# Eleven units' planes added on VectorE, filter weights loaded in two row groups, the last half tile in two parts, a zeroed tile for TensorE, and new order strings

## The chip, the cores and the metric

The kernel runs on one core of one Trainium2 chip. The core has five engines that run their own instruction queues in order and wait for each other through semaphores: TensorE (PE, matrix multiplications and transposes into PSUM), VectorE (DVE), ScalarE (ACT), GpSimd (POOL) and SyncE (SP, here the engine that issues nearly all DMA transfers). The metric is the device time of one execution in microseconds.

## The reference, cut to what matters

One block with two branches, batch 1, 2048 positions (S), 640 features (D), 1728 hidden features (F), all tensors bf16. The first branch is a spectral filter (a two-dimensional real Fourier transform over positions and features, a product with a complex weight, and the inverse), the second a gated feed-forward network. Both are modulated by six vectors that come from a condition `c`.

```python
mod = (silu(c) @ w_mod).reshape(1, 6, 1, 640)
sa, ca, ga, sb, cb, gb = (mod[:, i] for i in range(6))

h = layernorm(x) * (1 + ca) + sa
X = rfft2(h, axes=(1, 2)) * (w_r + 1j * w_i)       # [2048, 321] complex
x = x + ga * irfft2(X, s=(2048, 640), axes=(1, 2))

h = layernorm(x) * (1 + cb) + sb
x = x + gb * ((silu(h @ w_gate) * (h @ w_up)) @ w_down)
return x
```

## The kernel before, in words

The 2048 positions are 16 tiles of 128. The work has four stages, which follow each other on TensorE with some overlap. Inside the first three, the order of the work is written out by hand as a string (`plan`): each word is a step and a number, and the program issues the steps in that order, so that the string fixes the order on every engine's queue and on the DMA queue. PSUM is handed out in slots; the strings `SLOTS1` (three slots in stage 1) and `SLOTS2` (four slots afterwards) say which slot the next tile takes, and a matmul that writes a slot waits until the slot's last reader is done.

**Stage 1, forward transform.** For each tile `t` the steps are: `T` transposes x on TensorE (five 128x128 pieces), `h` copies them out, `G` forms sums of squares on TensorE, `d` (line 313) takes the statistics on VectorE, `p`/`r` root and reciprocal, `s` (line 333) scales a table `Gtab` on GpSimd, `B` multiplies with the table for the feature transform (line 340), `Z` (line 345) takes that out of PSUM on VectorE, `S` (lines 353, 354) does the position transform, `A` (line 367, tile 12 lines 362 to 364) copies the result to `A_sb`. At the end come the steps that prepare the weights and the shift: `ms`, `sacs`, `mh`, `sh` for the vector `sa`; `J`/`Je` (lines 438, 443) which reverse the weights on TensorE and copy them out to `Wq`; `N` (line 278) which negates three blocks on VectorE. The filter weights come in by `lW` (one DMA for each of the two tensors, 128 rows of 16x321), and `lf` (line 210) then overwrites parts of row 0 with eight small DMAs. `J` and `N` read the result.

**Stage 2, filter.** The transformed data are 17 units (0 to 16, the last one small). For a unit: `T`/`t` or a DMA transpose (`B`, `Bl`, line 487 and 492) brings `A_sb` into the order of the columns; `X` (lines 523 to 531) multiplies on TensorE for two units at a time, `Xe` (line 540; unit 16: line 536) copies it out of PSUM; `P` and `R` (both line 562) multiply with the weights on VectorE and leave two planes; `Y` turns the planes back on TensorE, `y` (line 599) copies it out; `E` (lines 611 to 624) multiplies on TensorE and `e` (line 634; half of unit 15 is `g15`) copies to `Ep`; `m` (line 278) writes negated mirror columns of `Ep` on VectorE.

For `Y` there are two ways. Without addition, TensorE multiplies each plane with the identity and sums both in PSUM: ten matmuls of 128 columns (lines 586 and 590), fp32 in PSUM. For the units in `ADDED`, VectorE adds the two planes first (`a`, line 570) and TensorE only transposes the sum: five transposes (lines 580 and 581), bf16 in PSUM.

Which engine copies a tile out of PSUM is decided by its name: names in `ON_DVE` go to VectorE, all others to ScalarE (`evict`).

**Stage 3, inverse transform and start of the network.** `s` (line 720), `V` (line 727), `d` (line 733) and `x` (line 736) undo the transform and form the residual x1; then come the second normalisation, its transposes, and for the first 512 positions the first eight of 13 blocks of the network (`g`, line 812, `z`, line 817, `m`, line 821). `w`, line 848, multiplies a row block of `w_down` with the gate; those blocks that are not in the string come in the loop behind it by `folds`.

**Stage 4, network.** Four groups of 512 positions, 13 blocks and a short 14th each, then the product with `w_down`: `down` (line 934) runs 13 matmuls into one accumulator of 128x320 for each half tile, `down13` (line 921) adds the short block, `x_out` (lines 946, 948) adds the residual and sends the tile out (lines 950, 952). The very last half tile has two accumulators of 160 columns; the residual is put into them by two identity matmuls (line 931), their matmuls alternate, and at the end ScalarE copies one and VectorE the other, and one DMA sends the 320 columns.

At the start TensorE waits for the first transfer (`c`), does five tiny matmuls with it (line 398) and twelve matmuls of the identity whose result is not used (line 400).

Of the kernel before, what the change touches and what calls it, by code (L numbers as in the profile page):

```python
# [30 lines left out]
def _tables():  # L31
# [79 lines left out]
def adaln_block_kernel(  # L111
# [39 lines left out]
    one11 = const.tile([1, 1], BF16, name="one11")  # L151
    identb = const.tile([P, 128], BF16, name="identb")
# [29 lines left out]
    g_row = [dram.tile([1, D], BF16, name=n) for n in ("ga_row", "gb_row")]  # L182
    nc.vector.memset(one11[:], 1.0)
# [34 lines left out]
    def load_g(g):  # L218
# [4 lines left out]
             "lW": lambda a: nc.sync.dma_start(Wb[:, a, :, 0:321], ws[a]), "lK": load(Ktab[:], K_dram), "lKI": load(KIt[:], KI_dram),  # L223
# [3 lines left out]
        "A12 Xe0 Xe9 Xe10 Xe16 e1 e14 e15 f0 f1 f2 f3 f4 f6 f7 f8 f9 g15 h0 t0 t1 y0 y2 y4 y8 y12 y14 y16 "  # L227
# [55 lines left out]
    with tc.tile_pool(name="ph1", bufs=3) as ph1, \  # L283
# [111 lines left out]

        cps = Tt[:, 330:330 + NC5]
        for k in range(NC5):
            nc.tensor.matmul(cps[:, k:k + 1], lhsT=c_row[0:1, k * 128:(k + 1) * 128], rhs=one11[:], start=True, stop=True)
        for _ in range(12):
            nc.tensor.matmul(Gt[:, 0:128], lhsT=identb[:], rhs=identb[:], start=True, stop=True)  # L400
# [44 lines left out]
        def negate(i):  # L445
# [30 lines left out]
    with tc.tile_pool(name="ph2", bufs=2, reuse_waits="tile") as ph2:  # L476
# [186 lines left out]
        def loads(i):  # L663
# [44 lines left out]
    def ring(name):  # L708
        return take2(name)
# [140 lines left out]
    def at_of(sc):  # L850
# [31 lines left out]
    folds = {8: (4, 5, 6), 9: (7,), 10: (8,), 11: (9, 10, 11), 12: (12, 13)}  # L882
    for sc in range(4):
# [3 lines left out]
        for fc in range(0 if sc else done, NFC - 1):  # L887
# [30 lines left out]
        def down13(tl, h):  # L918
            r = slice(64 * h, 64 * h + 64)
# [102 lines left out]
```

## Time and profile before

| | |
|---|---|
| median of 3 runs | 262.87 us (262.04 to 264.65) |
| the profiled execution, its own time | 262.81 us |
| span in the profile | 261.0 us |
| TensorE busy | 252.7 us (97%) |
| VectorE busy | 141.1 us (54%) |
| ScalarE busy | 118.6 us (45%) |
| GpSimd busy | 26.4 us (10%) |
| moved by DMA | 27.88 MB |

The profile is of one execution. Its span reaches from the first to the last recorded event; 1.8 us of the execution's time lie outside of it. The page has the busy time of each engine, the chain of work that ended last, followed back through what released each instruction, and the groups of instructions by line. The trace behind it can be asked for windows, for one engine's instructions in order of time, and for what each waited for. The ends of matmuls are modelled: a matmul's duration includes its way through the array, while the next one starts long before. So the step from one start to the next says what a matmul costs in a row.

### The profile page before, as it was taken

The numbers are of one execution on the slowest core, as the hardware profiler recorded it, in microseconds if no ns is written. First come the engines' busy times: TensorE is split into PE (matmuls) and PEld (weight loads), VectorE is DVE, ScalarE is ACT, GpSimd is POOL, SyncE is SP. The second block draws the span as 40 slices with busy tenths as digits, with TensorE's granted clock in tenths as the row PEclk, the third lists the DMA queues.
The fourth block names the chain that finished last, engine by engine and source line by source line (L and its number), as shares of the span: only waits on it lengthen the run. The fifth ranks groups of instructions, "written<-read, shape, count | busy, mean of one in ns | idle before, by whom it ended". The sixth has DMA issues, their size and how long they took to land.

```text
span 261.0 us, 5283 instructions
## 1 busy us (share of the span) xinstructions
PE 252.7 (97%) x2168; PEld 159.9 (61%) x2172; DVE 141.1 (54%) x353; ACT 118.6 (45%) x212; POOL 26.4 (10%) x57
## 2 busy tenths in 40 slices
PE   6899999999999999999999999999999999999995
PEld 5788666888995444466544456744445664444664
DVE  5799989999887664933243343234344322433122
ACT  5689879996993669420222222032223103222000
POOL 4289700000010001300000000000000000000000
PEclk9999999999999999999999999999999999999999
DMA  7999499999599100141100040210005011000011
GB/s 243 381 356 298 112 175 160 176 330 379 153 370 303 38 14 1 23 77 57 58 10 3 0 92 11 75 35 10 3 0 100 30 48 35 10 3 0 0 53 50
DMA packets 36798, 27.88 MB, mean 107 GB/s; under 512 B 19493, under 2 KB 34214, under 8 KB 36646
## 3 DMA queue, kind: packets, MB, share of 16 engines
q1 hardware_dynamic: 36762, 27.54, 37.1%
q8 instruction: 17, 0.28, 0.5%
q14 instruction: 7, 0.06, 0.1%
q10 hardware_dynamic: 12, 0.00, 0.0%
HBM read 20.13 MB, written 2.62 MB: 87 GB/s over the span
## 4 chain that ended last, share of the span: by engine, by line
PE 79%; DVE 12%; ACT 3%; issue 2%; DMA 2%; SPq 1%; DVEq 0%; ACTq 0%
PE gu L812 37%; PE oa L934 21%; PE va L720 3%; DVE PP L562 3%; DMA x_sb<-in_A_x_dram 2%; PE oab L733 2%; PE gu L799 2%; ACT junk L744 2%; PE aps L353 1%; DVE AT L821 1%; PE aps L354 1%; PE z L340 1%; DVE Z L345 1%; PE gps L308 1%; DVE late L848 1%
## 5 line engine op out<-in xcount | busy, mean ns | idle before, releaser
L821 DVE TENSOR_TENSOR AT<-gu,sg 128x512 bf16<-128x512 f32 x52 | 35.7, 690 | 63.3 <-ACT sg L817 63.3
L812 PE MATMUL gu<-h2T_all,Wg 128*128 128x512 bf16 x260 | 64.6, 379 | 0.1
L812 PE MATMUL gu<-h2T_all,Wu 128*128 128x512 bf16 x256 | 63.7, 379 | 0.1
L817 ACT ACTIVATE sg<-gu 128x512 f32<-128x512 f32 x52 | 30.7, 596 | 67.9 <-PE gu L812 65.1
L934 PE MATMUL oa<-late,AT 128*128 128x320 bf16 x403 | 56.3, 299 | 0.5 <-DVE AT L821 0.5
L934 PEld LDWEIGHTS <-AT 128*128 128x128 bf16 x429 | 40.7, 98 | 17.6 <-issue 1.1
L812 PEld LDWEIGHTS <-Wu 128*128 128x128 bf16 x260 | 25.4, 98 | 30.7
L812 PEld LDWEIGHTS <-Wg 128*128 128x128 bf16 x260 | 25.3, 98 | 29.9
L948 DVE TENSOR_TENSOR xo<-oa,late 128x320 bf16<-128x320 f32 x31 | 13.4, 484 | 34.6 <-PE oa L934 18.2
L801 ACT ACTIVATE sg<-gu 64x512 f32<-64x512 f32 x4 | 2.4, 591 | 36.0 <-PE gu L799 36.0
L736 DVE SCALAR_TENSOR_TENSOR late<-oab,x_sb 128x640 bf16<-128x640 f32 x16 | 12.8, 822 | 6.4 <-PE oab L733 5.0
L333 POOL TENSOR_SCALAR Gs<-Gtab,rstd 128x256 bf16<-128x256 bf16 x15 | 13.9, 928 | 8.1 <-DVE rstd L323 7.1
L345 DVE SCALAR_TENSOR_TENSOR Z<-rtile,vm,z 128x640 bf16<-128x640 f32 x16 | 13.9, 871 | 0.1
L744 ACT ACTIVATE junk<-late,mean 128x640 bf16<-128x640 bf16 x16 | 13.3, 828 | 0.3
L367 ACT CAST A_sb<-aps 128x650 bf16<-128x650 f32 x15 | 10.6, 706 | 2.1 <-PE aps L354 2.0
L727 ACT CAST VT<-va 128x640 bf16<-128x640 f32 x16 | 10.2, 699 | 1.9 <-PE va L720 1.8
L720 PE MATMUL va<-Htab,Ep 128*128 128x128 bf16 x160 | 10.6, 219 | 0.1
L720 PEld LDWEIGHTS <-Ep 128*128 128x128 bf16 x160 | 9.5, 118 | 0.4 <-DVE Ep L278 0.3
L353 PE MATMUL aps<-Z,Gs 128*128 128x325 bf16 x32 | 9.2, 303 | 0.2 <-DVE Z L345 0.2
L354 PE MATMUL aps<-Z,Gs 128*128 128x315 bf16 x32 | 9.2, 298 | 0.0
L540 ACT CAST X<-xps 128x640 bf16<-128x640 f32 x13 | 8.5, 710 | 1.1 <-PE xps L531 0.8
L562 DVE TENSOR_TENSOR PP<-X,Wb 128x768 bf16<-128x768 bf16 x16 | 8.7, 550 | 0.0
(291 smaller groups left out, 307.0 us busy)
## 6 DMA issues: line engine op xcount, KB each, us to landing
x_sb<-in_A_x_dram SPq DMA_DIRECT2D x8, 320.0 KB
out_dram<-xo SPq DMA_DIRECT2D x15, 160.0 KB, 2.2
Wu<-in_B_w_up_dram SPq DMA_DIRECT2D x1, 2080.0 KB
late<-in_B_w_down_dram SPq DMA_DIRECT2D x1, 2080.0 KB
wm_g<-in_w_mod_dram SPq DMA_DIRECT2D x2, 800.0 KB
Wb<-in_A_w_r_dram SPq DMA_DIRECT2D x1, 1284.0 KB
Wb<-in_A_w_i_dram SPq DMA_DIRECT2D x1, 1284.0 KB, 13.0
Wg<-in_B_w_gate_dram SPq DMA_DIRECT2D x1, 1280.0 KB, 8.1
```

Source lines behind the costliest of these rows:

```text
L333: e.tensor_scalar(Gss[t][:, 0:2], Gtab[:, t], rstd1[:, t:t + 1], None, ALU.mult)
L345: nc.vector.scalar_tensor_tensor(Zs[t][:].rearrange("p r q -> p (r q)"), rv, vm[:, t, 1:2], held.pop(("z", t))[:, 0:D], ALU.mult, ALU.add)
L353: nc.tensor.matmul(o, lhsT=Gs[:, a, :], rhs=Z[:, :, 0:NL], start=True, stop=False)
L562: nc.vector.tensor_tensor(bass.AP(o.tensor, o.offset, [o.ap[0], [4 * NI, 2], [2 * NI, 2], [4, n], [1, 4]]), bass.AP(xi.tensor, xi.offset, ...
L720: nc.tensor.matmul(vf[:, 128 * r:128 * r + 128], lhsT=Ep[:, t, 65 - 65 * g:193 - 65 * g, r], rhs=Htab[:, t, g, :], start=(f == 1 and r in ...
L736: nc.vector.scalar_tensor_tensor(x1[:, t, :].rearrange("p (a r) -> p a r", r=NR), VTs.pop(t).rearrange("p (r a) -> p a r", r=NR), 1.0, x_s ...
L744: nc.scalar.activation(junk[:], x1[:, t, :], ACT.Square, scale=-1.0 / D ** 0.5, bias=mean2[:, t, 1:2], accum_out=sq2[:, t:t + 1])
L812: nc.tensor.matmul(o, lhsT=w_[:, c5, fc * 128:(fc + 1) * 128], rhs=h2T(sc, c5), start=(c5 == 0), stop=(c5 == NC5 - 1))
L817: nc.scalar.activation(gus[fc][1][:], gus[fc][0][:, 0, :], ACT.Silu)
L821: nc.vector.tensor_tensor(AT[:, fc, :], gu[:, 1, :], sg[:], ALU.mult)
L934: nc.tensor.matmul(o, lhsT=AT[:, fc, tl * 128:(tl + 1) * 128], rhs=Wd_sb[:, fc, h * 320 + d0:h * 320 + d0 + n], start=(fc == 0 and not ear ...
L948: nc.vector.tensor_tensor(xos[tl][:, h * 320:(h + 1) * 320], ps[0][0], x_half(tl, h), ALU.add)
```

## The change

1. `ADDED` goes from eight units (0, 2, 4, 6, 8, 10, 12, 14) to eleven (1, 2, 4, 5, 6, 8, 9, 10, 12, 13, 14).
2. `ON_DVE` is another set. In stage 1, `A11` and `h3` are copied by VectorE instead of `A12` and `h0`. In stage 2 VectorE gives up `Xe0`, `Xe9`, `Xe10`, `Xe16`, `e1`, `e14`, the first half of `e15`, `y0` and `y8`, and takes `y1`, `y5`, `y6`, `y9`, `y10`, `y13`. In stage 3 `f4` goes to ScalarE and `f5` to VectorE.
3. The load of each filter weight tensor is split: `lw` loads rows 0 to 15, `lW` rows 16 to 127. Both `lw` stand ahead of `lsa`. The eight row fixes keep their form.
4. A tile `hot` of zeros is set by VectorE first of all; TensorE multiplies it nine times ahead of the five matmuls with `c`, and the twelve matmuls behind them use it in place of the identity.
5. The last half tile of the last group is two parts of 160 columns, one after the other, each with its 13 matmuls and its short block, its own addition of the residual on VectorE and its own DMA. The two identity matmuls are gone. The addition of the other half of that tile is now issued behind the first part's matmuls.
6. `folds` is spread otherwise; the last two blocks are multiplied behind the multiplication of block 12 instead of ahead of it.
7. The three order strings and the slot strings are new. Among other things the loads `lga`, `lKI` and `lRi` are issued in stage 1, `lga` ahead of the row fixes; the fixes of the second tensor (`lf4` to `lf7`) come ahead of those of the first; `J2` comes ahead of four `S` steps; `Xe0` and `Xe1` both run on ScalarE.

```diff
 SLOTS1 = (
-    "012021021021021020210210212012010210210210210"
+    "012021021021021021020120121021201201201201201"
...
+    nc.vector.memset(hot[:], 0.0)
...
-             "lW": lambda a: nc.sync.dma_start(Wb[:, a, :, 0:321], ws[a]), "lK": load(Ktab[:], K_dram), "lKI": load(KIt[:], KI_dram),
+             "lw": lambda a: nc.sync.dma_start(Wb[0:16, a, :, 0:321], ws[a][0:16]),
+             "lW": lambda a: nc.sync.dma_start(Wb[16:P, a, :, 0:321], ws[a][16:P]), "lK": load(Ktab[:], K_dram), "lKI": load(KIt[:], KI_dram),
...
-        "A12 Xe0 Xe9 Xe10 Xe16 e1 e14 e15 f0 f1 f2 f3 f4 f6 f7 f8 f9 g15 h0 t0 t1 y0 y2 y4 y8 y12 y14 y16 "
+        "A11 f0 f1 f2 f3 f5 f6 f7 f8 f9 g15 h3 t0 t1 y1 y2 y4 y5 y6 y9 y10 y12 y13 y14 y16 "
...
+        def keep_busy(ps, n):
+            for _ in range(n):
+                nc.tensor.matmul(ps[:, 0:128], lhsT=hot[:], rhs=hot[:], start=True, stop=True)
...
+        keep_busy(Tt, 9)
...
-        for _ in range(12):
-            nc.tensor.matmul(Gt[:, 0:128], lhsT=identb[:], rhs=identb[:], start=True, stop=True)
+        keep_busy(Gt, 12)
...
-            "lx0 lca0 T0 lR T1 h1 lca1 lx2 h0 lg0 G0 lx4 lg2 ca cb d0 T2 T3 lx6 h2 G1 lg4 lx8 lg6 rs rvp d1 G2 B1 h3 d2 T5 p0 rv Z1 "
-            "lx10 r0 T4 G3 B0 h5 d3 Z0 lg8 h4 s1 T7 B3 G4 s0 T8 T6 p2 lx12 d4 lg10 r2 h7 S1 lx14 Z3 h8 s2 G5 d5 lg12 B2 lg14 h6 T9 "
-            "G6 B5 A1 Z2 B4 h9 S0 lsa d6 Z4 lW1 G7 T10 s3 d7 A0 p4 lW0 r4 S3 h10 Z5 lK G8 B7 p6 T11 d8 r6 S2 s5 A3 G9 lf0 B6 Z7 d9 "
-            "h11 T12 s7 lf1 S5 s6 G10 A2 lf2 h12 p8 lf3 B8 s4 Z6 d10 T13 lf4 B9 Z8 A5 G11 S7 r8 s9 d11 h13 Z9 s8 A7 S6 G12 T14 d12 "
-            "lf5 B12 S4 p10 Z12 r10 s11 A6 lf6 h14 G13 lf7 d13 B11 Z11 s10 T15 A4 h15 B13 p12 S9 Z13 G14 ms0 r12 s12 S8 d14 A9 B10 "
-            "S11 G15 Z10 A8 ms2 d15 B14 S10 A11 ms3 s13 Z14 S12 B15 ms4 p14 r14 A10 ms1 A12 S13 Z15 J3 wm s15 A13 S15 J2 s14 sacs "
-            "N1 Je3 A15 N0 mh S14 sh Je2 J0 N2 A14 J1 Je1 Je0 "
+            "lx0 lca0 T0 h0 T1 lR G0 lca1 lx2 lg0 ca cb h1 T2 d0 T3 lx4 G1 rs d1 h2 lg2 rvp G2 B1 h3 T4 rv T5 d2 lx6 h4 lg4 p0 G3 "
+            "lx8 h5 lg6 Z1 B0 T6 h6 d3 G4 r0 p2 lx10 Z0 B2 lg8 T8 lx12 d4 T7 Z2 G5 h8 s1 lg10 B4 lx14 T9 r2 d5 lg12 Z4 S1 G6 lg14 "
+            "lw1 h7 B3 lw0 h9 s0 T10 p4 A1 S0 d6 G7 B5 h10 r4 A0 lsa lW1 Z3 s3 T11 d7 Z5 B6 p6 G8 lW0 h11 s5 S3 lK r6 lga s4 S5 d8 "
+            "G9 s7 Z6 T12 A3 d9 A5 lf4 B7 s2 S4 Z7 h12 G10 p8 B8 lf5 B9 T13 s6 A4 r8 d10 lf6 s8 G11 h13 Z8 d11 S7 S2 Z9 G12 T14 A7 "
+            "B10 lf7 d12 p10 s9 r10 B11 A2 Z10 G13 d13 h14 S8 S6 G14 T15 A8 A6 Z11 B12 s10 lKI S10 lRi d14 h15 p12 B13 Z12 r12 s11 "
+            "A10 G15 Z13 S9 B14 A9 s12 d15 Z14 lf0 ms0 S11 lf1 ms2 p14 A11 ms3 B15 J2 wm Je2 s13 ms4 r14 Z15 S12 ms1 s15 S13 s14 "
+            "sacs A12 N1 S15 J3 A13 mh lf2 N0 S14 A15 Je3 sh A14 lf3 N2 J0 Je0 J1 Je1 "
...
-        ADDED = (0, 2, 4, 6, 8, 10, 12, 14)
+        ADDED = (1, 2, 4, 5, 6, 8, 9, 10, 12, 13, 14)
...
-            "T0 t0 lga B2 T1 B4 Bl2 t1 X0 B6 Xe0 Xe1 ga P1 R0 X2 X4 P0 Xe2 Xe3 R1 a0 R2 Xe4 P2 Y1 lKI R3 Xe5 P3 X6 y1 R5 Xe6 Y0 Xe7 "
-            "Y3 a2 Y2 y0 y3 P5 B8 Bl8 E0 T16 y2 X8 e0 E2 R6 t16 P4 B12 R4 Xe8 P6 e2 Y5 Xe9 y5 a4 E1 a6 gt e1 E3 Y4 E5 y4 e3 e5 Y6 "
-            "P9 R9 E4 R7 B10 y6 X10 lRi P7 B14 e4 Xe11 Y9 y9 P8 Y7 E6 Xe10 R8 P10 R11 X12 P11 y7 e6 a8 L2 Xe12 Xe13 R10 X16 Y11 "
-            "Xe16 E9 P12 y11 X14 e9 Xe14 a10 Xe15 P16 R13 Y8 R12 Y10 y8 E11 y10 Y16 P14 e11 P13 E7 E8 gs y16 E16 E10 R14 a12 a14 e7 "
-            "R15 Y12 e16 e8 y12 Y13 P15 Y14 e10 y14 m1 L1 E12 Y15 y13 E14 L3 L4 E13 e12 m2 y15 m0 e14 e13 E15 e15 m3 m4 Ri "
+            "B4 T0 t0 T1 B2 Bl2 t1 B6 X0 Xe0 Xe1 P0 R0 X2 P1 Xe2 X4 Xe3 R1 Xe4 ga Y0 P2 R3 Xe5 y0 R2 X6 Xe6 Bl8 a1 P3 a2 T16 t16 B8 "
+            "Y1 Xe7 Y2 R5 gt y1 B10 P4 y2 Y3 X16 P5 X8 y3 Xe16 P6 R4 Xe8 Xe9 R6 a5 R8 X10 a6 Y5 y5 P8 E3 Xe10 E0 R9 a4 E2 a8 Xe11 "
+            "Y6 y6 e3 R7 Y8 e0 B14 e2 B12 P9 P7 X12 a9 P10 y8 Xe12 E5 Y4 Y7 Xe13 E1 e5 y4 Y9 R13 R10 y7 E4 e1 gs R11 P12 y9 E6 a10 "
+            "X14 e4 e6 Xe14 Y10 R12 P11 Xe15 E8 a12 Y11 y10 P14 e8 Y12 E9 E10 R14 y11 P16 L1 y12 P15 Y16 L2 E11 y16 R15 e9 L3 E7 "
+            "a14 P13 e10 Y15 e11 a13 Y14 e7 E12 Y13 y14 y13 E14 m0 y15 e12 E15 e14 m2 E13 e15 E16 L4 e13 e16 m1 m4 m3 Ri "
...
-    folds = {8: (4, 5, 6), 9: (7,), 10: (8,), 11: (9, 10, 11), 12: (12, 13)}
+    folds = {8: (4, 5), 9: (6, 7), 10: (8, 9), 11: (10, 11), 13: (12, 13)}
...
+            if sc == 0 and fc == NFC - 2:
+                for f in folds[13]:
+                    fold(f)
...
         if sc == 3:
-            acc[7] = [ring("ob")[:, 0, 0:160] for _ in range(2)]
-
...
+            acc[7] = acc[7][:, 0:160]
+            acc.append(ring("ob")[:, 0, 0:160])
...
         def parts(tl, h):
-            o = acc[2 * tl + h]
-            return [(o[q], 160 * q, 160) for q in range(2)] if isinstance(o, list) else [(o, 0, 320)]
...
+            k = 2 * tl + h
+            return [(acc[k], 0, 160, True), (acc[8], 160, 160, False)] if k == 7 and sc == 3 else [(acc[k], 0, 320, tl > 1)]
...
+        def down13(tl, h, part):
+            r, (o, d0, n, early) = slice(64 * h, 64 * h + 64), part
+            nc.tensor.matmul(o, lhsT=AT[r, 13, tl * 128:(tl + 1) * 128], rhs=Wd_sb[r, 13, h * 320 + d0:h * 320 + d0 + n],
+                             start=early, stop=not early)
...
+        def down(tl, h, part):
+            o, d0, n, early = part
             for fc in range(NFC - 1):
-                for o, d0, n in ps:
-                    nc.tensor.matmul(o, lhsT=AT[:, fc, tl * 128:(tl + 1) * 128], rhs=Wd_sb[:, fc, h * 320 + d0:h * 320 + d0 + n],
-                                     start=(fc == 0 and not early(tl, h) and len(ps) == 1), stop=(fc == NFC - 2 and early(tl, h)))
+                nc.tensor.matmul(o, lhsT=AT[:, fc, tl * 128:(tl + 1) * 128], rhs=Wd_sb[:, fc, h * 320 + d0:h * 320 + d0 + n],
+                                 start=(fc == 0 and not early), stop=(fc == NFC - 2 and early))
...
             if h == 0:
                 xos[tl] = ph4.tile([P, D], BF16, name="xo", bufs=3)
-            ps = parts(tl, h)
-            if len(ps) > 1:
-                for (o, d0, n), copy in zip(ps, (nc.scalar.copy, nc.vector.tensor_copy)):
-                    copy(xos[tl][:, h * 320 + d0:h * 320 + d0 + n], o)
-            else:
-                nc.vector.tensor_tensor(xos[tl][:, h * 320:(h + 1) * 320], ps[0][0], x_half(tl, h), ALU.add)
+            o, d0, n, _ = part
+            d0 += 320 * h
+            nc.vector.tensor_tensor(xos[tl][:, d0:d0 + n], o, x1[:, t, d0:d0 + n], ALU.add)
...
-                nc.sync.dma_start(out_v[:, t, h * 320:(h + 1) * 320], xos[tl][:, h * 320:(h + 1) * 320])
+                nc.sync.dma_start(out_v[:, t, d0:d0 + n], xos[tl][:, d0:d0 + n])
...
             for h in range(2):
-                down(tl, h)
-                if not early(tl, h):
-                    down13(tl, h)
-                if sc == 3 and tl == 3:
-                    x_out(tl, h)
-            if sc < 3 or tl == 2:
-                for h in range(2):
-                    x_out(tl, h)
+                down(tl, h, parts(tl, h)[0])
+            for h in range(2):
+                x_out(tl, h, parts(tl, h)[0])
+        if sc == 3:
+            part = parts(3, 1)[1]
+            down(3, 1, part)
+            down13(3, 1, part)
+            x_out(3, 1, part)
...
```

More of the change, by code (lines that the diff above doesn't have):

```diff
@@ L151, in adaln_block_kernel @@
     one11 = const.tile([1, 1], BF16, name="one11")
+    hot = const.tile([P, 128], BF16, name="hot")
     identb = const.tile([P, 128], BF16, name="identb")
@@ L908, in adaln_block_kernel, with x_out @@
         if sc == 3:
-            acc[7] = [ring("ob")[:, 0, 0:160] for _ in range(2)]
-        def early(tl, h):
-            return tl > 1 and not (sc == 3 and tl == 3 and h)
+            acc[7] = acc[7][:, 0:160]
+            acc.append(ring("ob")[:, 0, 0:160])
         def parts(tl, h):
-            o = acc[2 * tl + h]
-            return [(o[q], 160 * q, 160) for q in range(2)] if isinstance(o, list) else [(o, 0, 320)]
-        def down13(tl, h):
-            r = slice(64 * h, 64 * h + 64)
-            for o, d0, n in parts(tl, h):
-                nc.tensor.matmul(o, lhsT=AT[r, 13, tl * 128:(tl + 1) * 128], rhs=Wd_sb[r, 13, h * 320 + d0:h * 320 + d0 + n],
-                                 start=early(tl, h), stop=not early(tl, h))
-        def x_half(tl, h):
-            return x1[:, 4 * sc + tl, 320 * h:320 * h + 320]
-        def down(tl, h):
-            ps = parts(tl, h)
-            if len(ps) > 1:
-                for o, d0, n in ps:
-                    nc.tensor.matmul(o, lhsT=identb[:], rhs=x_half(tl, h)[:, d0:d0 + n], start=True, stop=False)
+            k = 2 * tl + h
[6 more added lines that the diff above has]
+            o, d0, n, early = part
             for fc in range(NFC - 1):
-                for o, d0, n in ps:
-                    nc.tensor.matmul(o, lhsT=AT[:, fc, tl * 128:(tl + 1) * 128], rhs=Wd_sb[:, fc, h * 320 + d0:h * 320 + d0 + n],
-                                     start=(fc == 0 and not early(tl, h) and len(ps) == 1), stop=(fc == NFC - 2 and early(tl, h)))
+                nc.tensor.matmul(o, lhsT=AT[:, fc, tl * 128:(tl + 1) * 128], rhs=Wd_sb[:, fc, h * 320 + d0:h * 320 + d0 + n],
+                                 start=(fc == 0 and not early), stop=(fc == NFC - 2 and early))
         xos = {}
-        def x_out(tl, h):
+        def x_out(tl, h, part):
             t = 4 * sc + tl
```

13 lines of the change are left out of this document (5 added, 8 removed), and 10 rows, old and new, of the table plan.

## The prediction

> **What bounds the kernel now.** I read the page's first part, then windows cut at the seams between the stages (where TensorE passes from one kind of work to the next), then the chain of waits, and in each stage the instructions in order of time. The page:
>
> ```profile
> span 261.0 us, 5283 instructions
> PE 252.7 (97%) x2168; PEld 159.9 (61%) x2172; DVE 141.1 (54%) x353; ACT 118.6 (45%) x212; POOL 26.4 (10%) x57
> ```
>
> The windows (from:to, length, then busy time of PE, weight loads, VectorE, ScalarE, GpSimd, granted clock, DMA share, GB/s):
>
> ```profile
> 9.67:35.62 25.95, 25.22 (x342) 20.69 (x339) 25.01 (x81) 22.63 (x40) 18.86 (x30) 1.00 0.86 266
> 35.08:62.72 27.64, 26.55 (x421) 21.93 (x420) 26.48 (x64) 25.05 (x43) 0.00 (x0) 1.00 1.01 238
> 64.20:112.22 48.02, 47.31 (x449) 30.30 (x454) 35.37 (x94) 33.96 (x69) 4.49 (x6) 1.00 0.44 135
> 112.22:250.53 138.31, 138.31 (x789) 74.89 (x790) 45.48 (x84) 31.36 (x51) 0.00 (x0) 1.00 0.11 29
> 258.15:261.00 2.85, 0.00 (x0) 0.00 (x0) 0.33 (x1) 0.23 (x1) 0.00 (x0) 1.00 0.10 29
> ```
>
> TensorE's 97% is two different things. From 112.22 to 250.53 it has no gap at all, and its instructions there are the same before and after: 138.3 us that nothing in this change can touch. In stage 1 (row 1) and stage 2 (row 2) VectorE is full, 25.01 of 25.95 and 26.48 of 27.64; ScalarE is close behind in stage 2 with 25.05. TensorE's busy time there, 25.22 and 26.55, counts the modelled tail of its matmuls, so it is less full than it looks. The chain of waits says the same of stage 2 (start, length, what):
>
> ```profile
> 50.90 0.73 DVE X L540
> ...
> 53.98 0.23 DVE X L536
> ...
> 56.22 0.40 DVE Y L599
> ...
> 58.09 0.80 DVE PP L570 x2
> ...
> 63.84 0.32 DVE Ep L278
> ...
> 64.20 1.59 PE va L720 x25
> ```
>
> The pieces between these are nearly all VectorE's too: it runs through VectorE up to the last mirror columns at 63.84, and only then TensorE begins stage 3 at 64.20. So an edit pays in stage 2 if it takes time off VectorE without filling ScalarE; it pays on TensorE itself only outside of stages 1 and 2.
>
> **The change part by part.**
>
> *Added planes and the new eviction sets (stage 2).* The prices, from VectorE's, ScalarE's and TensorE's instructions in order of time:
>
> ```profile
> 61.85 0.81 DVE L634 CAST Ep<-eps__1464 128x640 bf16<-128x640 f32 x1
> 62.65 0.50 DVE L634 CAST Ep<-eps__1490 128x320 bf16<-128x320 f32 x1
> 63.06 0.48 DVE L634 CAST Ep<-eps__1491 128x320 bf16<-128x320 f32 x1
> ...
> 39.03 2.48 ACT L540 CAST X<-xps 128x640 bf16<-128x640 f32 x4 [0.66 <-PE xps L531]
> 51.25 1.33 ACT L599 CAST Y<-yps 128x640 bf16<-128x640 f32 x2
> 57.30 0.75 ACT L634 CAST Ep<-eps__1362 128x640 bf16<-128x640 f32 x1
> 62.24 0.72 ACT L634 CAST Ep<-eps__1476 128x640 bf16<-128x640 f32 x1 [0.34 <-PE eps__1476 L624]
> ...
> 51.02 0.61 PE L586 MATMUL yps<-identb,PP 128*128 128x128 bf16 x8
> 48.90 0.22 PE L581 MATMUL yps<-identb,PP 128*128 128x128 bf16 x1
> ```
>
> VectorE gains three additions at 0.40 (two took 0.80) and, net, four Y copies at 0.40: +2.8. It loses three X copies at 0.73, the small one at 0.23, e1 and e14 at 0.80 (61.85 to 62.65) and half of e15 at 0.41: -4.4. Net -1.6 us. Not all of it counts: Xe0 stands at the opening, where VectorE waits for the first X anyway, so that its 0.73 is still spent, now as a wait for ScalarE. That leaves **-0.9**.
>
> ScalarE takes three X at 0.59 (2.48 less some 0.12 by which one copy's end overlaps the next, over 4), the small X (0.23 as on VectorE), e1 and e14 at 0.63 (0.75 less 0.12), half of e15 (0.41 as bound): +3.7. It gives four Y at 0.60 net: -2.4. Net +1.3, so 25.05 becomes 26.3.
>
> TensorE loses 3 x 5 matmuls of (0.61 - 0.22)/7 = 0.056, hence 0.84, but not on the path: it has gaps there now, and it waits for the two others. Its matmuls begin to count only if both others fall below it. I cost this part at 0; if the cover went, it would be another gain of at most 0.84.
>
> ScalarE would be the fuller queue then, 26.3 against 24.9 (26.48 - 1.6). But the two end differently: ScalarE's last copy now ends at 62.96, 1.2 us before stage 3 starts at 64.20, and behind it stand only the mirror columns, 0.32 to 0.4. ScalarE begins at 35.25 (below); with 26.3 of work, its present 2.6 us of waits (27.64 - 25.05) and the mirror it would let stage 3 start at 64.6: +0.4. Those waits were free so far, since VectorE was the later one, and the longest of those shown here, 0.66 and 0.34, are waits for TensorE. VectorE's own line gives -0.9, and -1.4 if half of its 1.2 us of waits go. I take **-0.8**, near VectorE's end, and keep -1.4 and +0.4 for the range.
>
> *Stage 1: order, weights in two row groups, A11/A12, h0/h3.* The swaps of copies are even. What ends the stage:
>
> ```profile
> 30.65 0.62 PE L438 MATMUL wps<-Wb,jrev 128*128 128x512 bf16 x2
> 35.25 1.93 ACT L443 CAST Wq<-wps 128x1024 bf16<-128x1024 f32 x2 [0.19 <-PE wps L438]
> 36.23 0.78 PE L523 MATMUL xps<-Ktab,B_all 128*128 128x160 bf16 x8 [0.43 <-DVE B_all L507]
> ...
> 26.23 2.58 SPq L210 DMA_DIRECT2D Wb<-in_A_w_i_dram  x4
> 28.86 0.40 SPq L213 DMA_DIRECT2D wm_g<-in_w_mod_dram  x1
> ...
> 24.00:25.00 1.00, 1.00 (x21) 1.00 (x19) 0.96 (x6) 0.87 (x3) 0.89 (x3) 1.00 0.98 319
> 25.00:26.00 1.00, 1.00 (x17) 0.83 (x15) 1.00 (x3) 0.96 (x3) 1.00 (x2) 1.00 0.29 93
> 34.00:35.00 1.00, 1.00 (x7) 0.48 (x5) 1.00 (x3) 0.74 (x2) 0.00 (x0) 1.00 0.99 187
> ```
>
> VectorE's instructions of 9.67 to 35.62 are the same but for the copies of even cost, so the stage can shrink by little more than its 0.9 us of gaps (25.95 - 25.01); TensorE's wait of 0.43 at 36.23 is for its last copies. Against that stands the weight reversal: `J2` now comes ahead of four S steps, where the first one, at 30.65, had two behind it. Between J2 and the first X copy ScalarE has four weight copies (0.9 each by the two in 1.93), A13 to A15 (0.59 each as X) and A12 in three parts (twice that): 6.6 us. They end at 37.06 now (35.25 + 1.93 less 0.12), and J2 itself takes 0.45 (0.62 less its tail), so J2 may start at 30.0 at the latest if nothing is to be lost. It needs the row fixes. They were issued at 26.23 to 28.8 because they waited for the whole weights; now they wait for rows 0 to 15 alone, but the 0.82 MB of `lga` (128 x 5 x 640 x 2 bytes), 2.6 us at 319 GB/s, are queued ahead of them. The big loads end at about 25.5 (the rate falls to 93 GB/s in that microsecond), so `lga` lands at 28.1 and the fixes soon after: ahead of 30.0, with 1 us or so to spare. `lga` was issued at 28.86 before and is a new burden only on what follows it; `lKI` and `lRi` stand behind `lf7` and ahead of `lf0` to `lf3`, which only the last two reversals need. No load waits for an engine ahead of the DMA transposes in either order. I put the stage at **-0.5**, from -1.2 to +1.0 (J2 one microsecond past its 30.0).
>
> *Folds.* One row pair:
>
> ```profile
> 111.56 0.61 DVE AT L821
> 112.22 5.61 PE oa L934 x40
> ```
>
> TensorE stood 0.49 us for block 12's multiplication, which stood behind two folds of 0.40. They now follow it. What is late next is the fold of block 12 itself, one 0.40 later, which the 13th of TensorE's matmuls needs: some 0.1 of the wait stays. **-0.35** (-0.5 to 0). The rest of stage 3 has the same instructions and TensorE nearly full; I cost its new order at 0 (-0.2 to +0.5).
>
> *The last half tile.*
>
> ```profile
> 256.08 1.80 PE ob L934 x26
> 257.88 0.25 PE ob L921 x2
> 258.15 0.33 DVE xo L946
> ...
> out_dram<-xo SPq DMA_DIRECT2D x15, 160.0 KB, 2.2
> out_dram<-xo SPq DMA_DIRECT2D x2, 80.0 KB, 1.6
> ```
>
> The matmuls cost 1.80/26 = 0.07. Two identity ones go (0.14) and one short one moves ahead of the half tile (0.07). The last addition is of 160 columns like the copy that it replaces, 0.33. The last store is 40 KB in place of 80; from 160 to 80 KB the landing fell by 0.6, but much of it is fixed. **-0.2** (-0.5 to +0.4). [...] As a mechanism of this kernel, a last store that lands like the 160 KB ones, 0.6 later, puts the tail at +0.4, and I keep that as a rival.
>
> *The zeroed tile.*
>
> ```profile
> 2.17 0.29 PE L398 MATMUL t1ps<-one,first_w 1*128 1x1 bf16 x5 [2.17 <-DMA first_w<-in_c_dram]
> 2.39 1.46 PE L400 MATMUL gps<-identb 128*128 128x128 bf16 x12
> ...
> 7.50 0.75 PE L301 MATMUL t<-identb,x_sb 128*128 128x128 bf16 x10 [0.28 <-DMA x_sb<-in_A_x_dram]
> ```
>
> The nine matmuls take 9 x 0.11 (1.46 less a tail of 0.17, over 12), about 1.0 us, inside the 2.17 that TensorE waits for `c`. Those twelve ran at half the later pace (0.11 against 0.056) although the granted clock is shown as 1.00. Earlier work may bring the full pace earlier, but the third tile waits for its x at 7.50, which no TensorE work moves: **0** (-0.5 to +0.2). [...]
>
> **The sum.** -0.8 - 0.5 - 0.35 - 0.2 = -1.85 against the execution's 262.81 (span 261.0 and 1.8 around it): 261.0. The median before is 262.87, so the two scales differ by 0.06 only.
>
> **The rivals.**
>
> *All queues close up.* Stage 2 reaches -1.4, stage 1 its gaps and a little more (-1.2), folds -0.5, tail -0.3: 259.4. For it: the orders are new in both stages. Against: no stage runs without waits now. Chance 0.2.
>
> *ScalarE becomes the bound.* Its in-order queue keeps all of its 2.6 us of waits: stage 2 at +0.4, stage 1 at 0, since the first X copy stands behind the same weight copies; folds and tail remain (-0.55): 262.7. The added planes then do nothing for the time. For it: all 17 X, 16 of the 17 e and half of the other stand on that queue. Against: TensorE, for which it waited, has 0.84 less to do. Chance 0.22.
>
> *The split weights come late (slower).* The 112-row loads (2 x 112 x 16 x 321 x 2 bytes, 2.3 MB) and `lga` move at the lower rate that the queue shows in the row of 34.00, 187 GB/s, in place of 319: the weights take 12.3 in place of 7.2 us and end at 30.6, `lga` at 35.0, and J2 starts there instead of at 30.0: +5.0 - 0.8 - 0.55, 266.5. From J2 at 31.35 on (30.0 + 1.35) the change is slower than before. For it: TensorE works in order, so that four S steps wait behind J2. Against: 112 rows are not much fewer than 128. Chance 0.12.
>
> *Small stores.* The tail at +0.4: 261.6. Chance 0.04.
>
> **How the numbers follow.** The forecast has the rest, 0.42. About 1% is what a measurement of this kernel can tell from no change; 260.2 and 265.5 are those bounds. Faster: the first rival (0.2) and a fifth of the forecast's own spread: 0.28. Slower: the third rival and a trace of the second's upper end: 0.13. The remaining 0.59 lies within. The range goes from the first rival's end, 259.4, to 264.2, where stage 1 and 2 stand at +1.0 and +0.4 and folds and tail give nothing; the third rival is left out.
>
> **What would show it.** Right: in the changed profile TensorE's first `va` of stage 3 starts near 62.9 (64.20 - 1.3), with VectorE's busy time in stage 2 down by 1.6 and ScalarE's up by 1.3; the first X near 35.7; no wait over 0.2 us at `oa` L934's first; less than 2.8 us from the last addition to the end. Wrong: `wps` waiting for a DMA; TensorE or VectorE idle in stage 2 with ScalarE named as the releaser; a first `va` after 64.2.

## The result, and the profile after

The changed kernel takes 275.05 us (median of six runs, 273.41 to 276.19) against 262.97 for the kernel before on the same chips (262.04 to 264.65): ratio 1.044, 95% interval 1.040 to 1.049. The forecast was 261.0, inside 259.4 to 264.2. The change is slower by 12 us, and the prediction was wrong.

The profiled execution took 273.67 us with a span of 271.9. From the page of the changed kernel, its first part and the lines of slices (40 slices of 6.8 us; busy tenths, granted clock in tenths, GB/s):

```profile
span 271.9 us, 5274 instructions
...
PE 254.8 (94%) x2164; PEld 161.0 (59%) x2164; DVE 139.8 (51%) x353; ACT 119.3 (44%) x216; POOL 26.5 (10%) x57
...
PE   8999219999999999999999999999999999999995
...
PEclk9999756999999999999999999999999999999999
...
GB/s 249 387 194 220 211 159 77 130 169 378 346 128 321 336 34 2 11 53 44 76 34 10 2 0 96 46 53 10 10 2 61 36 75 34 10 2 0 0 51 48
```

TensorE has a hole in the fifth and sixth slice and a lowered clock behind it; before, it was full there. The windows at the seams (from:to, length, busy time of PE, weight loads, VectorE, ScalarE and GpSimd, granted clock, DMA share, GB/s) say where the 10.9 us of span came from:

```profile
29.20:39.77 10.57, 0.03 (x2) 0.04 (x2) 1.70 (x5) 0.69 (x2) 1.69 (x4) 0.60 0.79 196
39.77:47.26 7.49, 7.49 (x65) 4.31 (x65) 3.91 (x9) 5.03 (x9) 0.00 (x0) 0.66 0.38 73
47.26:75.24 27.98, 26.68 (x432) 21.88 (x430) 25.78 (x67) 26.42 (x47) 0.00 (x0) 1.00 0.94 249
75.24:123.18 47.94, 47.65 (x458) 30.63 (x459) 35.63 (x95) 33.52 (x69) 4.60 (x6) 1.00 0.42 129
123.18:253.77 130.59, 130.59 (x731) 69.72 (x731) 44.79 (x83) 30.75 (x50) 0.00 (x0) 1.00 0.12 30
253.77:271.90 18.13, 15.09 (x127) 10.82 (x124) 4.30 (x10) 0.60 (x1) 0.00 (x0) 1.00 0.11 37
```

Stage 1 ends, with the first transposed B block, at 47.26 in place of 35.08: +12.18. From there to stage 3's first long run of `oa` matmuls it is 75.92 us (27.98 + 47.94) in place of 77.14: -1.22. The next 130.59 us are equal, and the end is 18.13 in place of 18.18. So all of the loss, and more, lies in stage 1. What TensorE waited for there, from the list of its waits (us in total, times, longest) and its instructions in order of time:

```profile
PE wps L445 <- DMA Wb<-in_A_w_i_dram: 10.5, 1, 10.5
...
39.77 1.01 PE L445 MATMUL wps<-Wb,jrev 128*128 128x512 bf16 x2 [10.54 <-DMA Wb<-in_A_w_i_dram]
```

It is `J2`, the first weight reversal, and it waits for the filter weights. Their loads, in the windows of the changed kernel (rows 0-15 move in the first, rows 16-127 in the second):

```profile
15.00:19.00 4.00, 4.00 (x58) 3.50 (x56) 3.89 (x16) 3.56 (x7) 3.92 (x7) 1.00 1.17 95
21.00:29.00 8.00, 8.00 (x109) 6.84 (x107) 7.82 (x25) 6.75 (x13) 7.86 (x13) 1.00 1.16 208
```

and of the kernel before, where one load carries all 128 rows:

```profile
17.00:25.00 8.00, 8.00 (x113) 7.13 (x112) 7.68 (x29) 7.31 (x15) 7.71 (x13) 1.00 1.10 343
```

The DMA engines are as busy (1.16 to 1.17 against 1.10) and move 95 and 208 GB/s in place of 343. SyncE shows the consequence (start, length, what; changed kernel):

```profile
14.66 8.79 SPq L226 DMA_DIRECT2D Wb<-in_A_w_i_dram  x1
23.49 7.13 SPq L215 DMA_DIRECT2D Ktab<-tab_K  x1
30.67 1.10 SPq L215 DMA_DIRECT2D wm_g<-in_w_mod_dram  x1
31.88 3.45 SPq L212 DMA_DIRECT2D Wb<-in_A_w_i_dram  x4
```

In these rows each transfer is issued when the one ahead of it has been. The second big load took 8.79 us to issue and the table behind it 7.13, where the kernel before has 5.61 and 3.61. So the row fixes, which no longer had to wait for the whole weights, were issued from 31.88 on, later than those of before (26.23 to 28.8), and `lga` ran ahead of them. The pages of the two profiles give the time from issue to landing for one big load of each kernel (its size, then the us), first before, then changed:

```profile
Wb<-in_A_w_i_dram SPq DMA_DIRECT2D x1, 1284.0 KB, 13.0
```

```profile
Wb<-in_A_w_r_dram SPq DMA_DIRECT2D x1, 1123.5 KB, 19.1
```

Issued at 13.12 and 13.54, they landed at about 26.1 and 32.6. The larger fixes of `J2`'s tensor took 7.6 us from issue to landing in the changed kernel, 2.1 before; from 31.88 on, that is 39.5, just ahead of the reversal's 39.77.

### The profile page after: what moved, and what is told of

It reads as the page before. It is cut to its first block, busy times and chain, and to the rows that moved or that the text cites. A ratio compares the mean times of both kernels' runs of the same rounds, so it can differ in the third digit from the quotient of the medians.

```text
span 271.9 us, 5274 instructions
## 1 busy us (share of the span) xinstructions
PE 254.8 (94%) x2164; PEld 161.0 (59%) x2164; DVE 139.8 (51%) x353; ACT 119.3 (44%) x216; POOL 26.5 (10%) x57
## 4 chain that ended last, share of the span: by engine, by line
PE 70%; DVE 1%; issue 0%; ACT 0%
PE gu L819 41%; PE oa L935 20%; PE va L727 3%; PE gu L806 2%; PE oab L740 2%; PE oa L929 1%; PE mg_ps L244 1%; PE h2ps L779 0%; PE ob L935 0%; DVE late L743 0%; ACT sg L824 0%; DVE late L855 0%; DVE xo L946 0%; PE ob L929 0%; PE gT_ps L256 0%
## 5 line engine op out<-in xcount | busy, mean ns | idle before, releaser
L819 PE MATMUL gu<-h2T_all,Wu 128*128 128x512 bf16 x260 | 64.6, 379 | 0.0
L935 PE MATMUL oa<-late,AT 128*128 128x320 bf16 (+1 forms) x416 | 57.1, 297 | 0.2 <-DVE late L855 0.2
L819 PEld LDWEIGHTS <-Wu 128*128 128x128 bf16 x260 | 25.5, 98 | 30.7
L946 DVE TENSOR_TENSOR xo<-oa,late 128x320 bf16<-128x320 f32 (+1 forms) x32 | 13.7, 479 | 36.0 <-PE oa L935 19.1
L445 PE MATMUL wps<-Wb,jrev 128*128 128x512 bf16 x8 | 3.0, 492 | 10.5 <-DMA Wb<-in_A_w_i_dram 10.5
L370 ACT CAST A_sb<-aps 128x650 bf16<-128x650 f32 x14 | 9.6, 704 | 2.5 <-PE aps L357 2.5
L547 ACT CAST X<-xps 128x640 bf16<-128x640 f32 x16 | 10.3, 700 | 0.9 <-PE xps L538 0.9
L357 PE MATMUL aps<-Z,Gs 128*128 128x315 bf16 x32 | 10.3, 331 | 0.0
L356 PE MATMUL aps<-Z,Gs 128*128 128x325 bf16 x32 | 10.3, 333 | 0.0
```

The source lines that it names most:

```text
L356: nc.tensor.matmul(o, lhsT=Gs[:, a, :], rhs=Z[:, :, 0:NL], start=True, stop=False)
L357: nc.tensor.matmul(o[:, :, 1:64], lhsT=Gs[:, b, :], rhs=Z[:, :, NL:128], start=False, stop=True)
L819: nc.tensor.matmul(o, lhsT=w_[:, c5, fc * 128:(fc + 1) * 128], rhs=h2T(sc, c5), start=(c5 == 0), stop=(c5 == NC5 - 1))
L935: nc.tensor.matmul(o, lhsT=AT[:, fc, tl * 128:(tl + 1) * 128], rhs=Wd_sb[:, fc, h * 320 + d0:h * 320 + d0 + n], start=(fc == 0 and not ear ...
L946: nc.vector.tensor_tensor(xos[tl][:, d0:d0 + n], o, x1[:, t, d0:d0 + n], ALU.add)
```

## The experiments

All times and landmarks in one table: median time, ratio to the kernel before, run beside it on the same chip, with its 95% interval, start of the first reversal (`wps`), start of the first transposed block (T0, the end of stage 1), and the time from there to stage 3's first run of 40 `oa` matmuls. The times are medians of 4 to 12 executions (6 for the changed kernel), the landmarks are of one profiled execution each. The kernels ran on several chips, so they are compared by their ratios.

| kernel | us | ratio | reversal | T0 | T0 to `oa` |
|---|---|---|---|---|---|
| before | 262.97 | 1 | 30.65 | 35.08 | 77.14 |
| changed | 275.05 | 1.044 (1.040-1.049) | 39.77 | 47.26 | 75.92 |
| e1 whole loads | 262.26 | 0.998 (0.995-1.000) | 30.42 | 35.67 | 76.12 |
| e2 split only | 274.14 | 1.040 (1.034-1.046) | 40.13 | 45.70 | 77.13 |
| e3 rows by 4 | 261.94 | 0.994 (0.991-0.996) | 29.48 | 34.74 | 76.17 |
| e4 blocks of 32 | 275.20 | 1.046 (1.042-1.050) | 40.74 | 48.28 | 76.01 |
| e5 kept warm | 275.13 | 1.047 (1.044-1.051) | 40.74 | 45.99 | 78.23 |
| e6 planes, gate load late | 267.30 | 1.015 (1.011-1.018) | 30.62 | 35.06 | 81.69 |
| e7 rows by 2 | 262.29 | 0.997 (0.995-0.999) | 31.37 | 36.62 | 76.06 |
| e8 before, rows by 4 | 263.78 | 1.003 (1.001-1.005) | 32.56 | 36.99 | 76.53 |
| e9 planes | 263.34 | 1.001 (0.998-1.004) | 31.71 | 35.45 | 77.40 |
| e10 to rows by 4 | 261.83 | 0.994 (0.991-0.998) | 29.20 | 34.46 | 76.12 |
| e11 to blocks | 274.35 | 1.041 (1.037-1.045) | 40.96 | 48.68 | 76.04 |
| e12 quarter first | 261.88 | 0.995 (0.992-0.998) | 30.27 | 35.53 | 76.08 |
| e13 planes, loads ahead | 262.50 | 0.997 (0.995-1.000) | 30.69 | 35.12 | 76.42 |
| e14 loads ahead | 263.36 | 1.000 (0.997-1.002) | 31.05 | 35.48 | 77.10 |

**Undo the split, and make it alone (e1, e2).**

On the changed kernel (e1), where the steps `lw1` and `lw0` go from the plan too:

```diff
-"lw": lambda a: nc.sync.dma_start(Wb[0:16, a, :, 0:321], ws[a][0:16]),
-"lW": lambda a: nc.sync.dma_start(Wb[16:P, a, :, 0:321], ws[a][16:P])
+"lW": lambda a: nc.sync.dma_start(Wb[:, a, :, 0:321], ws[a])
```

On the kernel before (e2) the same lines the other way round, and in its plan:

```diff
-S0 lsa d6
+S0 lw1 lw0 lsa d6
```

Theory A in the expectations is that the split loads are slow in themselves (95 and 208 GB/s in place of 343, as above), rival B that the new order makes the loss.

> The changed kernel, but each filter weight is loaded whole, in one DMA of 128 rows, and not as rows 0-15 and 16-127; order, planes, tail and zeroed tile stay as changed. [...] Rival B (the new order is what hurts: the 0.8 MB gate weights and a reversal ahead of four S steps): the rate is high, but the first reversal still waits 3 us or more, and the time is 265 or above.

> The kernel before, with one thing of the change: the weights are loaded as rows 0-15 and rows 16-127, the two small loads issued just ahead of the sa weights, as in the change. Theory A: 76 to 130 GB/s during the 16-row loads and 170 to 235 during the 112-row loads; the big loads end at 31 to 34 us in place of 25.5, the first reversal waits for a DMA by 2 to 4 us, and the time is 265 to 268 us. Rival B: the loads end within 1 us of where they did and the time is within 1 us of 262.9.

The split alone costs 11 us on the kernel before; without it the change is no slower than before. In e2 the order is the old one, so rival B (the order) falls. The loss was larger than I expected of e2. From its list of waits, its windows, and SyncE's instructions in order of time:

```profile
PE wps L439 <- DMA Wb<-in_A_w_i_dram: 8.9, 1, 8.9
```

```profile
15.00:19.00 4.00, 4.00 (x54) 3.40 (x52) 3.89 (x15) 3.24 (x7) 3.16 (x7) 1.00 1.20 104
21.00:29.00 8.00, 8.00 (x109) 6.87 (x107) 7.68 (x28) 6.76 (x13) 7.88 (x15) 1.00 1.16 203
```

```profile
34.75 4.47 SPq L210 DMA_DIRECT2D Wb<-in_A_w_i_dram  x4
```

The rates are the expected ones. What I had left out is SyncE's queue: the fixes that the first reversal needs stand behind the loads there and were issued from 34.75 on, to 39.2.

**Few rows, or the wrong rows? (e3, e4, e7).** Four loads of 32 rows each in e3 and e4, which differ only in which rows go together, and two of 64 in e7:

```diff
-"lW": lambda a: nc.sync.dma_start(Wb[:, a, :, 0:321], ws[a])
+"lW": lambda a: [nc.sync.dma_start(Wb[j:P:4, a, :, 0:321], ws[a][j:P:4]) for j in range(4)]
```

That is e3, on e1. In e4 both `j:P:4` read `32 * j:32 * j + 32`; in e7 they read `j:P:2`, for two values of `j`.

> As the kernel with whole weight loads, but each weight comes in four DMAs of 32 rows, rows j, j+4, j+8 and so on. [...] Rival C ('fewer rows, or several DMAs, are slow in themselves'): the rate falls to 230 GB/s or less, as with blocks of 32 rows, and the first reversal waits for 5 us or more.

> As the kernel with whole weight loads, but each weight comes in four DMAs of 32 neighbouring rows, so that number and size of the DMAs are those of the kernel with rows four apart and only the rows' places differ. [...] Rival C: same rate and same time as with rows four apart.

> As the kernel with rows four apart, but each weight in two DMAs of 64 rows, the even and the odd ones. [...] Rival C (splitting costs by itself): 264 or above.

The same stretch of e3's windows, and of e4's:

```profile
17.00:25.00 8.00, 8.00 (x104) 6.82 (x102) 7.79 (x28) 6.58 (x13) 8.00 (x14) 1.00 1.12 336
```

```profile
17.00:25.00 8.00, 8.00 (x104) 6.81 (x102) 7.79 (x29) 6.53 (x13) 8.00 (x14) 1.00 1.19 156
```

Same number of loads, same rows per load, 336 against 156 GB/s. Neither few rows nor several loads were slow in e3, so rival C falls. e4 took 275.20 us, as long as the changed kernel. e7 has nearly e3's rate (319 to 329 GB/s); its reversal waited 1.2 us, and it took 262.29 us, where rival C had 264 or above.

**The memory on the chip or the weight's own? (e10, e11).** In e3 and e4 the rows stand apart, or together, on both sides of the transfer. The crosses tell the sides apart: `Wb[j:P:4] <- ws[a][32 * j:32 * j + 32]` (e10) and `Wb[32 * j:32 * j + 32] <- ws[a][j:P:4]` (e11).

> As the kernel with whole loads, each weight in four DMAs of 32 rows, but crossed: 32 neighbouring rows of the weight's memory go to rows four apart on the chip, so the weights' rows stand in another order (the work is the same, the values are not the reference's). If the place on the chip decides the rate: above 300 GB/s and 261 to 263 us, as with rows four apart on both sides. If the place in the weight's own memory decides: 140 to 200 GB/s and 272 to 276.

> The other cross: rows four apart of the weight's memory go to 32 neighbouring rows on the chip (again the rows stand in another order than the reference's). If the place on the chip decides: 140 to 200 GB/s, the first reversal waits some 11 us and the time is 272 to 276 us. If the weight's memory decides: above 300 GB/s and 261 to 263.

The windows of e10, then of e11:

```profile
17.00:25.00 8.00, 8.00 (x104) 6.82 (x102) 7.79 (x28) 6.58 (x13) 8.00 (x13) 1.00 1.11 345
```

```profile
17.00:25.00 8.00, 8.00 (x104) 6.81 (x102) 7.79 (x28) 6.59 (x13) 8.00 (x13) 1.00 1.20 151
```

The place of the rows on the chip decided, and their place in the weight's own memory made no such difference: 345 GB/s in e10 and 336 in e3, 151 in e11 and 156 in e4. How many rows go together does not give the rate: 16 neighbouring rows moved at 95 to 104 GB/s, 32 at 151 to 156, rows 16 to 127 at 203 to 208 and all 128 at 343, but 32 rows four apart at 336 to 345. Why the neighbouring rows are slow, rows 16 to 127 among them, is not shown by any run here.

**The early rows taken from everywhere (e12).** The changed kernel with its early part kept, of other rows:

```diff
-"lw": lambda a: nc.sync.dma_start(Wb[0:16, a, :, 0:321], ws[a][0:16]),
-"lW": lambda a: nc.sync.dma_start(Wb[16:P, a, :, 0:321], ws[a][16:P])
+"lw": lambda a: nc.sync.dma_start(Wb[0:P:4, a, :, 0:321], ws[a][0:P:4]),
+"lW": lambda a: [nc.sync.dma_start(Wb[j:P:4, a, :, 0:321], ws[a][j:P:4]) for j in (1, 2, 3)]
```

> The changed kernel with its two-part loads kept in their places, but the early part of each weight is the rows 0, 4, 8 and so on in place of 0 to 15, and the rest comes as the three other quarters. Theory A: above 300 GB/s until all is in, the row fixes wait for the early quarter alone, the first reversal waits less than 0.5 us, and the time is 261.2 to 262.2 us, ratio to before 0.993 to 0.998. If the two small loads ahead of the sa weights or the eight issues cost something of their own, 263 or above.

As forecast in time, with a wait of 0.95 in place of 0.5 us at the reversal and 259 to 297 GB/s in the microseconds 22 to 27. e3 and e12 lie a little below both kernels: e3 0.4 to 0.9% and e12 0.2 to 0.8% below before.

**Is e3's gain that of its loads? (e8).** The kernel before with `lW` as in e3.

> The kernel before with one thing altered: each weight in four DMAs of rows four apart. Its first reversal did not wait for a DMA, so if the gain of the changed order with such loads over before (ratio 0.9935) comes from the planes, the order and the folds, this one stays within 0.5 us of before. Rival: the gain is the loads' own; then it comes out 0.8 us or more below before.

Not by themselves: on the kernel before they make it 0.3% slower, 0.96 us, more than the 0.5 that I had allowed. Its profile lost 1.9 us in stage 1, 0.56 of it at the third tile, which waited for its `x` (8.06 in place of 7.50); what the rest is stays open.

**What the clock costs (e5).** 188 matmuls on the zeroed tile ahead of `J2`, `... B15 K188 J2 wm` with `"K": lambda n: keep_busy(Gt, n)`.

> The changed kernel as it is (split loads), with 188 matmuls on the zeroed tile put ahead of the first reversal, so that TensorE is busy during its wait of 10.5 us. Theory A with the clock: the reversal still starts near 39.8 us, but the granted clock stays at 1.00, from the reversal to the first transposed B block it takes 5.3 us as with whole loads in place of 7.5, and the time is 272.4 to 273.4 us, some 2 below the changed kernel's 275.05. Rival D (the 2.2 us between are the late row fixes or ScalarE's copies and not the clock): the stretch stays at 7 us or more and the time within 0.5 us of 275.05.

The windows of e5 (reversal to T0, then T0 to stage 3, then a stretch within) and its next wait:

```profile
40.74:45.99 5.25, 5.25 (x64) 3.57 (x65) 3.70 (x9) 4.61 (x9) 0.00 (x0) 1.00 0.29 55
45.99:76.27 30.28, 27.95 (x431) 22.70 (x429) 26.17 (x67) 26.59 (x47) 0.00 (x0) 0.94 0.90 239
...
50.00:53.00 3.00, 3.00 (x46) 2.00 (x45) 1.80 (x5) 1.61 (x3) 0.00 (x0) 0.50 1.02 195
```

```profile
49.55 1.08 PE L530 MATMUL xps<-Ktab,B_all 128*128 128x160 bf16 x8 [1.36 <-DMA B_all<-A_sb]
```

The stretch after the wait shrinks from 7.49 to 5.25 us at clock 1.00, so 2.24 us of the loss there were the clock, as theory A had it. But the time did not move: the X products come earlier than the DMA transposes that they need, TensorE waits 1.36 us for one, and the clock halves after all, from 49.8 to 53.2. The 2.24 us were given back further on, where it is 2.31 more (78.23 against 75.92); besides, the reversal began 0.97 later in e5's profile (40.74 against 39.77). So the expected 2 us came in one place and not in the sum.

**The planes by themselves (e6, e9, e13, e14).** On the kernel before, stage 2's `ADDED`, eviction sets, order and slots of the change; the loads `lga`, `lKI`, `lRi`, which stand in stage 2 before and in stage 1 after the change, had to be given places.

In e6 they were put back into the change's plan:

```diff
-B4 T0 t0 T1
+B4 T0 t0 lga T1
...
-Y0 P2 R3
+Y0 P2 lKI R3
...
-X10 a6
+X10 lRi a6
```

e9 begins with `lga B4 T0 t0 T1` instead. e13 begins with `lga lKI lRi B4 T0 t0 T1` and has no load further on. e14 is the kernel before with its own stage 2, which begins with `T0 t0 lga lKI lRi B2` and has no load further on.

> The kernel before with the stage-2 part of the change alone: eleven units' planes added, the new eviction sets of stage 2, its new order and its slots; the three loads that stand in stage 2 keep their places; stages 1 and 3, loads, tail and start are those of before. By the recorded sum: VectorE's busy time in stage 2 down by 1.6 us, ScalarE's up by 1.3, the stretch from the first transposed block to the first long output product shorter by 0.8 us (between 1.4 shorter and 0.4 longer), the time 0.8 below before. Rival (ScalarE becomes the bound): the stretch within 0.3 us of before's 77.1 or longer.

e6 measured my own placing of a load, not the planes. From its instructions in order of time:

```profile
40.40 0.85 PE L523 MATMUL xps<-Ktab,B_all 128*128 128x160 bf16 x5 [3.12 <-DMA B_all<-A_sb]
```

`lga` between the first two DMA transposes held the second one up, TensorE waited 3.12 us, and its clock was 0.50 from 40 to 46.

> As the kernel with the planes alone, but the 0.8 MB gate load is issued ahead of the first DMA transpose and not between the first and the second, where it held up the second (TensorE waited 3.1 us for it at the second pair of X products and its clock halved). Two readings of the earlier loss of 4.5 us: that the place of the load made it, then the stretch from the first transposed block to the first long output product comes to 76.3 to 76.8 us (77.14 before, folds not being part of this kernel) and the time to 0.3 to 0.9 below before; or that the planes and the new order are slower by themselves, then it stays above 79.

> The kernel before with the stage-2 part alone, as in the kernel with the gate load first, and the two small loads of stage 2 (280 and 160 KB) also moved ahead of the first DMA transpose, where the change has them. If the planes need the queue free of loads between the transposes to bring their gain: no X product waits over 0.4 us for a transpose, the stretch from the first transposed block to the first long output product is 76.2 to 76.7 us, and the time is 0.4 to 1.0 below before. If the planes bring nothing by themselves: 77.0 or more, and the time within 0.3 of before.

> The kernel before with those two small loads moved ahead of the transposes and nothing else. If the moved loads alone make the gain: the stretch is 76.2 to 76.7 us and the time 0.4 to 1.0 below before. If they only make room for the planes: the stretch within 0.3 us of 77.1 and the time within 0.3 us of before.

The stretch from T0: 77.14 before, 77.40 with the planes, 77.10 with the loads ahead, 76.42 with both. Neither does it alone. e9 lies between the two readings of its expectation. In it two X products still wait for a transpose; its list of waits, then that of e13:

```profile
PE xps L523 <- DMA B_all<-A_sb: 0.7, 1, 0.7
...
PE xps L531 <- DMA B_all<-A_sb: 0.5, 1, 0.5
```

```profile
PE xps L531 <- DMA B_all<-A_sb: 0.3, 1, 0.3
```

The planes take VectorE's time away, and then the transposes set the pace, unless no load stands between them. That is my reading of one profile of each; in time e9 and e13 are not told apart (their intervals overlap). e13's time is 0.6 us below before (0 to 0.5%).

## Why the prediction was wrong, and where it was right

**Stage 1 failed** (-0.5 forecast, +12.18 measured). The step that failed is "they wait for rows 0 to 15 alone ... The big loads end at about 25.5": I took the loads' end from the kernel before, as if the split left their rate alone. One of them landed at about 32.6 instead, rows 0 to 15 having moved at 95 GB/s and the rest at 208 in place of 343; the fixes, and with them `J2`, came 9.8 us later than the 30.0 that I had allowed for `J2`. e2 shows that the split alone makes the loss, and e10 and e11 that the chip's side of the transfer makes it. Of the 12.18, the first reversal's delay is 9.12 (39.77 against 30.65). The other 3.06 is the stretch from there to T0, 7.49 against 4.43: 2.24 of it the halved clock (e5), 0.82 the steps that the new order puts behind `J2` (5.25 with whole loads as well).

**The third rival had the mechanism and not the size.** It had `J2` at 35.0 and 266.5 us, with 0.12. That its rate for the 112-row loads, 187 GB/s, came near the measured 208 is luck: in the row of 34.00, from which it was taken, the queue had no load left, only the DMA transposes that SyncE had issued from 31.89 on. Three terms were missing or too small. It gave rows 0 to 15 no time of their own, but they moved at 95. It let the fixes land right behind `lga`, at 35.0, but SyncE could issue them only from 31.88 on and the larger ones then took 7.6 us, to 39.5. It had no term for the clock. What I set against it, "112 rows are not much fewer than 128", is the wrong measure: 32 rows four apart ran at 336 to 345 GB/s, and 112 neighbouring ones at 203 to 208.

**Stage 2 was right, for a reason half told.** Stage 2 of the kernel before, from T0 to its first `va`:

```profile
35.08:63.65 28.57, 27.48 (x447) 22.77 (x446) 27.41 (x66) 25.28 (x43) 0.00 (x0) 1.00 1.01 244
```

VectorE's 27.41 us became 25.78 and ScalarE's 25.28 became 26.42: -1.63 and +1.14 against the -1.6 and +1.3 of the sum. The stretch fell by 0.86: 64.20 less the 0.28 of five `va` that before ran ahead of it gives 28.84, now 27.98. In seven other kernels with this stage 2 and unhurt transposes it is 28.07 to 28.21. So -0.6 to -0.9 against -0.8. ScalarE did become the fuller engine without becoming the bound, so the second rival did not occur. But e9 and e13 (77.40 and 76.42 us from T0 to `oa`) point to a second condition, the loads out of the transposes' way, which the prediction booked as a burden only.

**The folds** (-0.35): stage 3 up to `oa` is 47.94 against 48.30 (48.02 and the 0.28), and TensorE's wait at `oa` is 0.2 in place of 0.5. Right.

**The last half tile** (-0.2): from the last long run of `oa` to the end, the kernels with the old tail take 18.12 to 18.36 and those with the new one 17.89 to 18.13, in the mean 0.2 less. From the last addition's start to the end it is 2.77 to 3.00 with the new and 2.79 to 3.04 with the old: the stores of 320-byte rows land neither earlier nor 0.6 later, so that rival did not occur, and the gain is that of the matmuls. "Less than 2.8" was too narrow, at 3.00 in the changed kernel.

**The zeroed tile** (0): the third tile starts at 7.59 (7.50 before), and the twelve matmuls behind `c` still take 1.46. Right, and the full pace did not come earlier in this profile: the matmuls of the first two tiles take 0.73 and 0.74, five each, and the ten of the third 0.75, all as before. The -0.5 at the end of its range is shown by no run: the third tile started 0.09 later, not sooner.

With loads that keep their rate the sum has the right sign, but it is too large: e1, e3, e7, e10 and e12 lie 0.5 to 1.7 us below the kernel before beside them (medians), where 1.85 was forecast. Stage 1 is where they differ most from the sum: e1's stage 1 ended 0.6 later than before, where -0.5 was forecast, and e3's 0.34 earlier.

## What to carry to other kernels

Before a load is split, ask which rows go together, not only how many. Early rows that are needed soon are better taken from the whole height (every fourth row): here blocks of 16, 32 and 112 neighbouring rows moved at 95 to 208 GB/s, 32 rows four apart (e3, e10) at 336 to 345, and the DMA engines looked as busy, with a share of 1.1 to 1.2 in both. The slow loads cost three times: by themselves, by all that stood behind them in the queue that issued them (the fixes from 31.88 on in place of 26.23), and by the clock that TensorE lost in the wait (2.24 us). Removing work from the full engine paid, by my reading of e9 and e13, only where the next thing in line, here the DMA transposes, could follow.

## What the runs showed of the hardware that I had not expected

The rate of a load into the chip went by the places of its rows: 95 to 104 GB/s for 16 neighbouring rows (means of 4 us, the last of which has part of the next load; 76 to 93 in the three before it in the changed kernel), 151 to 156 for 32, 203 to 208 for rows 16 to 127, 336 to 345 for 32 rows four apart and 343 for all, at a DMA share of 1.1 to 1.2 in each case.

Where the first reversal waited long, the granted clock fell 2.0 to 3.9 us after TensorE's last instruction. In the changed kernel that ended at 29.23; its windows:

```profile
31.00:32.00 1.00, 0.00 (x0) 0.00 (x0) 0.00 (x0) 0.00 (x0) 0.13 (x1) 0.63 1.09 220
...
44.00:45.00 1.00, 1.00 (x6) 0.36 (x5) 0.86 (x2) 0.62 (x2) 0.00 (x0) 0.54 0.81 161
```

Between 1.00 and 0.50, a mean of 0.63 puts the fall near 31.3, and 0.54 the return near 44.9, 5.1 us after work had begun again at 39.77. In e2, e4 and e11 the fall came 2.8, 3.0 and 3.9 us after the last instruction and the return 4.1, 5.2 and 5.6 us after work had begun again; in e5 it fell after a wait of 1.36 us, in a stretch with several gaps, and came back 3.6 us after that wait.

In all six runs the clock stayed halved for a multiple of 3.41 us. Worked out from its mean in windows of 0.05 us, that is 13.65 us in the changed kernel, e4 and e11, 10.24 in e2, 6.83 in e6 and 3.41 in e5: four, three, two and one times 3.41. No experiment tested why. TensorE was busy throughout the last 3.41 us before the return in each of them; in e6 the 3.41 us before those held 2.74 us of work, and the clock stayed halved. The 3.41 us that ended with the fall held 1.38 us of work in the changed kernel and 1.74 in e5.
